# Two transformer layers on one core: polynomial and shifts moved from GpSimd to VectorE, shifts in pairs, single P buffers, a longer opening of layer 2

## The chip, the cores and the metric

The kernel runs on one core of a Trainium2 chip. The metric is the device time of one execution in microseconds, median of three runs. The core has five engines: TensorE (PE, matmuls; PEld its weight loads), VectorE (DVE), ScalarE (ACT), GpSimd (POOL) and SyncE (SP, which issues the DMAs).

## The reference

Two identical layers work on x of 2048 rows by 512, in bf16. Each is self-attention with 32 heads of 16 columns and then a feed-forward part of width 1792, both behind a layer norm without weights:

```
x = x + A(layernorm(x));  x = x + B(layernorm(x))        # twice
A(x): q, k, v = split(x @ wqkv);  softmax(q k^T / 4) v, heads joined, @ wo
B(x): gelu_tanh(x @ w1 + b1) @ w2 + b2
```

## The kernel before, in words

Keys and queries lie transposed, 128 columns (8 heads) to a block, and scores are computed transposed: 128 keys by 512 queries for one head. Such a **cell** fills one bank of PSUM (512 f32 a partition). There are 2 layers x 4 query chunks x 32 heads x 16 key tiles = 4096 cells. A **pass** is one query chunk, one block of columns and one of its two head halves, so four heads, and 64 cells where it takes all 16 key tiles; four matmuls of 32 rows each run side by side (`score`, L872). `qpad` (L860) masks the queries of a pass on GpSimd.

Most cells go to ScalarE: `exps` (L992) takes groups of three and two banks in turn and writes exp of them to a P buffer (L1004). Before, there are five P buffers of three cells, and a buffer is free when all its cells have been used. Some cells go to VectorE instead, only from four key tiles per layer (`KD`, L31): `dcell` (L962) turns a score into the bits of a bf16 number by one multiply-add to uint16 (L970). Three more copies of it, shifted by 32, 64 and 96 of these units, come from one shift of 512 elements (L973) and one of 1024 (L981 on VectorE, or for every third cell, if the planner sees GpSimd free, L978 there). The four are summed by four value matmuls with weighted copies of V (`VC`, made by `vcopies`, L845, on GpSimd), where a cell of ScalarE needs one. Before, five places (`DU`) hold the four forms of one cell each. `pvs` (L1020) runs the value matmuls of a pass into one bank, four heads side by side, and frees P buffers and places; `norm` (L603) transposes the sum, divides by its row of sums, and transposes back.

When a chunk's attention is done, `post` (L763) runs its output projection (`wo`, L637), a layer norm (`ln`, L473), seven pairs of hidden blocks (`hpair`, L692), the second product (`ytile`, L738) and, in layer 1, the next layer norm and the K, V, Q of layer 2 (`projections`, L575), all beside the attention of later chunks. A pair is 8 matmuls into two banks (L704), two evacuations (L717), then the tanh form of Gelu on 1024 elements: on GpSimd a square (L728), a scaling (L729) and a product (L731); tanh on ScalarE (L732); on VectorE +1 (L733) and the last product (L734). The last chunk of layer 2 uses ScalarE's own Gelu (L712). Pairs are released by the count of scored cells (`when`, L760: a share of `span`). Weights come in pieces of 256 KB through a ring of buffers `WR` (`wloads`, L664): two for the output projection, seven for the pairs, and six for K, V, Q of layer 2.

The order of passes (L802) is written out. Layer 2 opens with eight passes of its first chunk over 12 key tiles, whose sums wait in `PART`; then come the last four key tiles, which need K and V of the last 512 rows. So the last chunk's feed-forward part in layer 1 and its projections have to be done by then.

The order on each engine is fixed when the program is built: a planner (`_Sched`, L183) keeps a clock for each engine, and among steps that are ready takes the one with the lowest priority number. Each step has an estimated cost. Scores have 0, value matmuls 1, VectorE steps that read PSUM 0.4 at most, exponentials 6, cells of VectorE 9, feed-forward 10 to 15. On the chip each engine then works through its list in that order, and waits for semaphores where a step depends on another engine, or on its own engine's earlier step (TensorE's apart).

Of the kernel before, what the change touches and what calls it, by code (L numbers as in the profile page):

```python
# [5 lines left out]
ALU = mybir.AluOpType  # L6
# [28 lines left out]
PTLOW = 1  # L35
# [281 lines left out]
def bass_interleave_layers__mha_block__dense_activation_gelu__prompt_kernel(  # L317
# [15 lines left out]
    with ExitStack() as es:  # L333
# [17 lines left out]
        T["X2"] = sb([128, 2, 1024], F16, "x2")  # L351
        T["PT"] = sb([128, PT_RING, CELLS, 512], BF16, "pt")
        T["PART"] = [v[:, 0:8192].bitcast(F32).rearrange("p (g q) -> p g q", g=8) for v in vf[::-1]]
        T["DU"] = sb([128, DU, 4, 512], U16, "du")
# [52 lines left out]
DV = 0.62  # L407


class _Plan:  # L410
# [62 lines left out]
    def ln(self, c, dst, dkeys, prio):  # L473

        T = self.T
        tiles = range(4 * c, 4 * c + 4)
        sl = slice(4 * c, 4 * c + 4)
        for t in tiles:
            yield ("need", ("xready", t, self.phase[c]))
            yield _Op("dve", 0.6, lambda e, t=t: e.bn_stats(T["STATS"][:, t, :], T["X"][:, t, :]),  # L480
                      reads=["X.%d" % t], writes=["ST.%d" % t])
            yield _Op("dve", 0.1, lambda e, t=t: e.bn_aggr(T["MV"][:, t, :], T["STATS"][:, t, :]),
                      reads=["ST.%d" % t], writes=["MV.%d" % t])
# [12 lines left out]
    def ln_tile(self, c, t, dst, dkeys):  # L496
        T = self.T
        x = yield ("acq", "xln")
        yield _Op("dve", 0.22, lambda e: e.tensor_scalar(
# [103 lines left out]
    def norm(self, l, qc, g, b, part, final):  # L603
# [3 lines left out]
        key = "B.%d" % b  # L607
        if not final:
            yield _Op("dve", DV, lambda e: e.tensor_copy(T["PART"][l][:, g, :], pv), reads=[key],
                      writes=["PART.%d.%d" % (l, g)] + (["V0.%d" % k for k in range(self.NT)] + ["V01"] if l else []))  # L610
            yield ("rel", "pv", b)
            return
        xt = T["XT"]
        if part:
            yield _Op("dve", DV, lambda e: e.tensor_tensor(out=T["PART"][l][:, g, :], in0=T["PART"][l][:, g, :], in1=pv, op=ALU.add),
                      reads=[key, "PART.%d.%d" % (l, g)], writes=["PART.%d.%d" % (l, g)])
            yield ("rel", "pv", b)
            yield _Op("dve", 0.68, lambda e: e.transpose(xt[:, :], T["PART"][l][:, g, :]), reads=["PART.%d.%d" % (l, g)], writes=["XT"])
        else:
            yield _Op("dve", 0.70, lambda e: e.transpose(xt[:, :], pv), reads=[key], writes=["XT"])  # L620
            yield ("rel", "pv", b)
        x3 = xt[:, :].rearrange("p (k c) -> p k c", c=32)
        yield _Op("dve", 0.2, lambda e: e.reciprocal(T["RC"][:, :].rearrange("p (k o) -> p k o", o=1), x3[:, :, 16:17]),
# [5 lines left out]
        yield _Op("dve", 0.35, lambda e: e.tensor_tensor(  # L629
            out=o3, in0=x3[:, :, 0:16], in1=T["RC"][:, :, None].to_broadcast([128, 16, 16]), op=ALU.mult),  # L630
            reads=["XT", "RC"], writes=okey)
        if gt == 1:
            yield _Op("dve", 0.68, lambda e: e.transpose(T["OTN"][:, gb, :], T["OTT"][:, o, :]),
                      reads=["OTT.%d.0" % o, "OTT.%d.1" % o], writes=["OTN.%d" % gb])
            yield ("give", ("otn", l, qc, gb))
# [56 lines left out]
    def hpair(self, l, c, p):  # L692
# [40 lines left out]
        yield _Op("dve", 0.34, lambda e: e.tensor_scalar(x2, x2, 1.0, None, op0=ALU.add), reads=xk, writes=xk)  # L733
# [68 lines left out]
    def passes(self):  # L802


        NT = self.NT
        out = []
        for l in range(NL):
            cut = 4 if l == 0 else NT - 4
            out += [(l, 0, g, range(cut), False, False) for g in range(8)]
            out += [(l, 0, g, range(cut, NT), True, True) for g in range(8)]  # L810
            for qc in range(1, self.NQ):
                out += [(l, qc, g, range(NT), False, True) for g in range(8)]
        return out
# [9 lines left out]
    def setup_attention(self):  # L823
# [18 lines left out]
        self.ptleft = {}  # L842
        self.turn, self.lend = 0, 2
# [16 lines left out]
    def qpad(self):  # L860
        T = self.T
        for pi, (l, qc, g, kts, part, final) in enumerate(self.pas):
# [3 lines left out]
            yield _Op("pool", 0.9, lambda e, s=s, b=b, t=t, qc=qc: e.tensor_scalar(  # L866
# [42 lines left out]
    def scores(self):  # L909
        u = 0  # L910
        pools = self.s.pools
        while True:
# [12 lines left out]
            while len(work) < 4 and (pools["dbank"] or len(pools["misc"]) > KEEP) and pools["du"]:  # L925
                d = self.next_d(used)
                if d is None:
                    break
# [3 lines left out]
                extra.append((d, b, pools["du"].pop(0), home))  # L932
# [29 lines left out]
    def dcell(self, cell, b, du, home):  # L962


        T = self.T
        pi, kt, a = cell
        l, _, g = self.pas[pi][:3]
        D4 = T["DU"][:, du, :, :]
        key = ["DU.%d.%d" % (du, i) for i in range(4)]
        yield _Op("dve", 0.68, lambda e: e.tensor_scalar(D4[:, 0, :], self.bank(b), E_SCALE, E_BIAS, op0=ALU.mult, op1=ALU.add),  # L970
                  reads=["B.%d" % b], writes=key[:1])
        yield ("rel", "dbank", b)
        yield _Op("dve", 0.20, lambda e: e.tensor_scalar(D4[:, 1, :], D4[:, 0, :], SHIFT, None, op0=ALU.add),  # L973
                  reads=key[:1], writes=key[1:2])
        lo, hi = D4[:, 0:2, :].rearrange("p j q -> p (j q)"), D4[:, 2:4, :].rearrange("p j q -> p (j q)")
        self.turn = (self.turn + 1) % 3
        if self.turn == 0 and self.s.clock["pool"] < self.s.clock["dve"] + 0.1:
            yield _Op("pool", 1.36, lambda e: e.tensor_scalar(hi, lo, 1.0, 2.0 * SHIFT, op0=ALU.mult, op1=ALU.add),  # L978
                      reads=key[:2], writes=key[2:])
        else:  # L980
            yield _Op("dve", 0.34, lambda e: e.tensor_scalar(hi, lo, 2 * SHIFT, None, op0=ALU.add), reads=key[:2],  # L981
                      writes=key[2:])
        h = 8 * (g // 2) + 2 * a + (g % 2)
        j = KD[l].index(kt)
        for i in range(4):
            if i == 0:
                w, wk = T["V"][l][:, kt, h, 0:17], ["V%d.%d" % (l, kt), "V%d1" % l]
            else:
                w, wk = T["VC"][:, j, i - 1, 17 * h:17 * h + 17], ["VC.%d.%d" % (j, i - 1)]
            self.dq[(pi, a)].append((w, D4[:, i, :].bitcast(BF16), wk + key[i:i + 1], du if i == 3 else None, i == 3, kt))  # L990

    def exps(self):  # L992
        T = self.T
        u = 0
        while True:
            got = yield ("need", ("s", u))
            if got is None:
                break
            sl, cells = got
            r = yield ("acq", "pt")  # L1000
            n = len(cells)
            src = self.bank(SLOTS[sl][0], n)
            dst = T["PT"][:, r, 0:n, :].rearrange("p j q -> p (j q)")
            yield _Op("act", 0.065 + 0.4267 * n, lambda e, src=src, dst=dst: e.activation(  # L1004
                out=dst, in_=src, func=ACT.Exp, scale=0.25),
                reads=["B.%d" % b for b in SLOTS[sl][:n]], writes=["PT.%d" % r])
            self.ptleft[r] = n
            for j, (pi, kt, a) in enumerate(cells):
                l, _, g = self.pas[pi][:3]
                h = 8 * (g // 2) + 2 * a + (g % 2)  # L1010
                self.aq[(pi, a)].append((T["V"][l][:, kt, h, 0:17], T["PT"][:, r, j, :],
                                         ["V%d.%d" % (l, kt), "V%d1" % l, "PT.%d" % r], r, True, kt))
# [7 lines left out]
    def pvs(self):  # L1020
        T = self.T
        pools = self.s.pools
        for pi, (l, qc, g, kts, part, final) in enumerate(self.pas):
# [8 lines left out]
            def ready(cols=cols):  # L1032
# [4 lines left out]
                if not pools["pt"] and any(self.aq[k] for k in cols):  # L1037
# [3 lines left out]
            while any(self.pvleft[k] for k in cols):  # L1041
                yield ("cond", ready)
                fns, reads, rounds, back = [], [], 0, []
                while rounds < ROUNDS:
# [6 lines left out]
                    for k in wide:  # L1051
# [10 lines left out]
                        if buf is not None:  # L1062
                            back.append(("pt" if q is self.aq[k] else "du", buf))
                yield _Op("pe", ST + MM * (rounds - 1), fns, reads=reads, writes=["B.%d" % b])
                for pool, r in back:
                    if pool == "pt":
                        self.ptleft[r] -= 1
                        if self.ptleft[r]:
# [5 lines left out]
    def run(self):  # L1074
# [12 lines left out]
        s.pool("x2", range(2))  # L1087
# [44 lines left out]
```

## Time and profile before

| | |
|---|---|
| median of 3 runs | 1902.27 us (1902.13 to 1907.1) |
| profiled execution | 1901.61 us, of which 1899.6 us from first to last instruction (span) |
| busy: ScalarE, TensorE, VectorE, GpSimd | 1653.7, 1553.3, 1342.6, 540.3 us |
| mean granted TensorE clock | 0.889 of full |

A line of a group names the kernel's line, the engine, the operation, the tiles out<-in with their shapes and the count; then the busy time in us (overlaps counted once), the mean ns of one, and the idle time of the engine before them with what ended it. A row of the windows has the stretch, its length, the busy us of PE, PEld, DVE, ACT and POOL with their instructions in brackets, the granted clock, the DMA share and GB/s.

### The profile page before, as it was taken

The numbers are of one execution on the slowest core, as the hardware profiler recorded it, in microseconds if no ns is written. First come the engines' busy times: TensorE is split into PE (matmuls) and PEld (weight loads), VectorE is DVE, ScalarE is ACT, GpSimd is POOL, SyncE is SP. The second block draws the span as 40 slices with busy tenths as digits, with TensorE's granted clock in tenths as the row PEclk, the third lists the DMA queues.
The fourth block names the chain that finished last, engine by engine and source line by source line (L and its number), as shares of the span: only waits on it lengthen the run. The fifth ranks groups of instructions, "written<-read, shape, count | busy, mean of one in ns | idle before, by whom it ended". The sixth has DMA issues, their size and how long they took to land.

```text
span 1899.6 us, 28436 instructions
## 1 busy us (share of the span) xinstructions
PE 1553.3 (82%) x11548; PEld 372.8 (20%) x11548; DVE 1342.6 (71%) x2561; ACT 1653.7 (87%) x1458; POOL 540.3 (28%) x450
## 2 busy tenths in 40 slices
PE   7988887889869897787977968878887797877976
PEld 2211111122212121121211211212111121111212
DVE  6475678865897668867579544898668866788662
ACT  6999997899969998699987969979998799977992
POOL 3111125411262113522246101352214511254110
PEclk9997788899989999789988985989888798997998
DMA  5100000001100011000110010100001000010001
GB/s 144 34 1 1 1 23 28 12 1 45 29 28 7 17 30 35 28 1 12 45 28 23 1 43 3 29 28 12 7 12 34 17 10 4 18 29 17 12 1 44
DMA packets 85150, 42.45 MB, mean 22 GB/s; under 512 B 34589, under 2 KB 85022, under 8 KB 85022
## 3 DMA queue, kind: packets, MB, share of 16 engines
q1 hardware_dynamic: 85022, 40.65, 7.9%
q8 instruction: 92, 1.51, 0.3%
q14 instruction: 36, 0.29, 0.1%
HBM read 30.68 MB, written 2.10 MB: 17 GB/s over the span
## 4 chain that ended last, share of the span: by engine, by line
ACT 46%; PE 26%; DVE 24%; issue 2%; DMA 1%; POOL 0%; SPq 0%; POOLq 0%
ACT pt L1004 46%; PE ps L1058 10%; PE ps L880 8%; DVE du L970 5%; DVE du L973 5%; DVE du L981 4%; PE ps L704 3%; DVE g L717 3%; PE ps L745 3%; DVE x L733 2%; DVE g L734 2%; PE ps L549 1%; DMA xf<-xln 1%; DVE ott L629 1%; DVE xt L620 1%
## 5 line engine op out<-in xcount | busy, mean ns | idle before, releaser
L1004 ACT ACTIVATE pt<-ps 128x1536 bf16<-128x1536 f32 x1385 | 1595.8, 1293 | 186.7 <-PE ps L880 137.7
L880 PE MATMUL ps<-qp,kt 32*128 32x512 bf16 x4096 | 596.8, 420 | 220.6 <-ACT pt L1004 151.2
L970 DVE TENSOR_SCALAR du<-ps 128x512 uint16<-128x512 f32 x633 | 429.1, 684 | 280.1 <-PE ps L880 273.9
L1058 PE MATMUL ps<-pt,v 128*17 128x512 bf16 x3463 | 560.1, 421 | 7.3 <-ACT pt L1004 2.8
L978 POOL TENSOR_SCALAR du<-du 128x1024 uint16<-128x1024 uint16 x173 | 184.7, 1068 | 824.9 <-DVE du L973 813.0
L1058 PE MATMUL ps<-du,vc 128*17 128x512 bf16 x1899 | 389.5, 431 | 1.6 <-DVE du L973 1.3
L880 PEld LDWEIGHTS ps<-qp,kt 32*128 32x128 bf16 x4096 | 144.1, 92 | 860.2 <-ACT pt L1004 461.9
L981 DVE TENSOR_SCALAR du<-du 128x1024 uint16<-128x1024 uint16 x460 | 249.7, 546 | 8.3
L973 DVE TENSOR_SCALAR du<-du 128x512 uint16<-128x512 uint16 x633 | 246.0, 397 | 11.7
L704 PE MATMUL ps<-xf,wr 128*128 128x512 bf16 x448 | 146.8, 439 | 80.9 <-DVE g L717 59.8
L1058 PE MATMUL ps<-du,v 128*17 128x512 bf16 x633 | 198.2, 431 | 10.5 <-DVE xt L620 6.9
L866 POOL TENSOR_SCALAR qp<-q,mask 128x512 bf16<-128x512 bf16 x80 | 58.4, 731 | 297.6 <-PE ps L880 288.0
L1058 PEld LDWEIGHTS ps<-pt,v 128*17 128x17 bf16 x3463 | 104.5, 88 | 187.8 <-issue 156.1
L728 POOL TENSOR_TENSOR x<-g 128x1024 f16<-128x1024 bf16 x49 | 95.3, 1945 | 135.3 <-DVE g L717 127.5
L745 PE MATMUL ps<-w,g 128*128 128x512 bf16 x448 | 128.4, 390 | 3.0 <-DVE du L970 3.0
L731 POOL TENSOR_TENSOR x<-x,g 128x1024 f16<-128x1024 f16 x49 | 109.9, 2243 | 3.9
L717 DVE TENSOR_SCALAR g<-ps,hb1t 128x512 bf16<-128x512 f32 x98 | 72.7, 742 | 28.6 <-PE ps L704 28.1
L1058 PEld LDWEIGHTS ps<-du,vc 128*17 128x17 bf16 x1899 | 74.8, 91 | 88.2 <-issue 71.4
L704 PEld LDWEIGHTS ps<-xf,wr 128*128 128x128 bf16 x448 | 33.0, 103 | 163.9 <-issue 86.2
L729 POOL TENSOR_SCALAR x<-x 128x1024 f16<-128x1024 f16 x49 | 54.5, 1113 | 4.3
L733 DVE TENSOR_SCALAR x<-x 128x1024 f16<-128x1024 f16 x49 | 53.9, 1099 | 0.8 <-ACT x L732 0.8
L732 ACT ACTIVATE x<-x 128x1024 f16<-128x1024 f16 x49 | 51.8, 1057 | 1.6 <-POOL x L731 1.5
(57 smaller groups left out, 719.9 us busy)
## 6 DMA issues: line engine op xcount, KB each, us to landing
wr<-in_B_w_dram SPq DMA_DIRECT2D x56, 256.0 KB, 2.9
wr<-in_A_wqkv_dram SPq DMA_DIRECT2D x24, 256.0 KB, 2.7
wr<-in_A_wo_dram SPq DMA_DIRECT2D x16, 256.0 KB, 2.7
x<-in_A_x_dram SPq DMA_DIRECT2D x4, 512.0 KB, 8.5
out_dram<-x SPq DMA_DIRECT2D x16, 128.0 KB, 1.7
w<-in_B_w_dram SPq DMA_DIRECT2D x1, 1792.0 KB, 10.8
g<-in_A_wqkv_dram SPq DMA_DIRECT2D x3, 512.0 KB, 6.3
xf<-xln SPq DMA_TRANSPOSE x48, 2.4
```

The lines of the kernel that those rows point to most:

```text
L704: fns = [lambda e, dc=dc, j=j, pb=pb: e.matmul(pb, lhsT=T["WR"][:, w, 256 * dc + 128 * j:256 * dc + 128 * j + 128], rhs=T["XF"][:, dc, :], ...
L717: yield _Op("dve", DV, lambda e, fc=fc, pb=pb: e.tensor_scalar(T["G"][:, fc, :], pb, T["HB1T"][:, fc:fc + 1], 0.5, op0=ALU.add, op1=ALU.mult),
L728: yield _Op("pool", 2.2, lambda e: e.tensor_tensor(out=x2, in0=g2, in1=g2, op=ALU.mult), reads=gk, writes=xk)
L731: yield _Op("pool", 2.2, lambda e: e.tensor_tensor(out=x2, in0=x2, in1=g2, op=ALU.mult), reads=gk + xk, writes=xk)
L745: fns = [lambda e, fc=fc: e.matmul(pb, lhsT=T["G"][:, fc, q], rhs=T["W2"][:, fc, :], start=(fc == 0), stop=False) for fc in range(NFC)]
L880: return (lambda e: e.matmul(o, lhsT=lhsT, rhs=rhs, start=True, stop=True, tile_position=(32 * a, 0)), ["K%d.%d.%d" % (l, g // 2, kt // 4) ...
L970: yield _Op("dve", 0.68, lambda e: e.tensor_scalar(D4[:, 0, :], self.bank(b), E_SCALE, E_BIAS, op0=ALU.mult, op1=ALU.add), reads=["B.%d" % ...
L973: yield _Op("dve", 0.20, lambda e: e.tensor_scalar(D4[:, 1, :], D4[:, 0, :], SHIFT, None, op0=ALU.add), reads=key[:1], writes=key[1:2])
L978: yield _Op("pool", 1.36, lambda e: e.tensor_scalar(hi, lo, 1.0, 2.0 * SHIFT, op0=ALU.mult, op1=ALU.add), reads=key[:2], writes=key[2:])
L981: yield _Op("dve", 0.34, lambda e: e.tensor_scalar(hi, lo, 2 * SHIFT, None, op0=ALU.add), reads=key[:2], writes=key[2:])
L1004: yield _Op("act", 0.065 + 0.4267 * n, lambda e, src=src, dst=dst: e.activation(out=dst, in_=src, func=ACT.Exp, scale=0.25), reads=["B.%d" ...
L1058: fns.append(lambda e, o=o, lhsT=lhsT, rhs=rhs, a=a, st=not begun[a], sp=self.pvleft[k] == 0: e.matmul(o, lhsT=lhsT, rhs=rhs, start=st, st ...
```

## The change

The square, scaling and product of Gelu are issued on VectorE instead of GpSimd, and GpSimd makes no double shifts. VectorE's cells are gathered in pairs: `dfirst` does the multiply-add of each cell, and `dchain`, with priority 16, waits until two cells are there (or no second can come, or the exponentials lack P buffers), then does one shift for both and one double shift for both. There are three pair places. A place is free when both its cells have been used. P has 15 single buffers; `units` finds two or three free ones at equal steps, which one exponential writes, and each is freed by itself. `PTLOW` (free P buffers at which the value matmuls turn to ScalarE's cells first) counts singles now. Layer 2 opens with 12 passes over 12 key tiles (eight of chunk 0, four of chunk 1, whose sums lie in the first layer's K), then their last four tiles; its key tiles for VectorE are 0, 1, 2 and 12. The weight ring has three buffers. Some estimated costs of the planner are changed.

```diff
-CELLS = 3
-PT_RING = 5
+PT_RING = 15
-W_RING = 5
+W_RING = 3
-DU = 5
-KD = ((4, 5, 6, 7), (0, 1, 2, 3))
+X2_RING = 2
+DU = 3
+PAIR = 2
+LAST = 450
+EARLY = 4
+KD = ((4, 5, 6, 7), (0, 1, 2, 12))
-PTLOW = 1
+PTLOW = 3
...
+        T["PT"] = sb([128, PT_RING, 512], BF16, "pt")
+        T["PART1"] = T["K"][0][:, :, :].rearrange("p c s -> p (c s)").bitcast(F32).rearrange("p (g q) -> p g q", g=8)
+        T["DU"] = sb([128, DU, 4, PAIR, 512], U16, "du")
...
-        yield _Op("pool", 2.2, lambda e: e.tensor_tensor(out=x2, in0=g2, in1=g2, op=ALU.mult), reads=gk, writes=xk)
-        yield _Op("pool", 0.8, lambda e: e.tensor_scalar(x2, x2, 8.0 * C2, 2.0 * C1, op0=ALU.mult, op1=ALU.add),
+        yield _Op("dve", 0.62, lambda e: e.tensor_tensor(out=x2, in0=g2, in1=g2, op=ALU.mult), reads=gk, writes=xk)
+        yield _Op("dve", 0.36, lambda e: e.tensor_scalar(x2, x2, 8.0 * C2, 2.0 * C1, op0=ALU.mult, op1=ALU.add),
                   reads=xk, writes=xk)
-        yield _Op("pool", 2.2, lambda e: e.tensor_tensor(out=x2, in0=x2, in1=g2, op=ALU.mult), reads=gk + xk, writes=xk)
+        yield _Op("dve", 0.62, lambda e: e.tensor_tensor(out=x2, in0=x2, in1=g2, op=ALU.mult), reads=gk + xk, writes=xk)
...
+        out = run(0, 0, range(8), range(4), False, False) + run(0, 0, range(8), range(4, NT), True, True)
+        for qc in range(1, self.NQ):
+            out += run(0, qc, range(8), every, False, True)
+        out += run(1, 0, range(8), most, False, False) + run(1, 1, range(EARLY), most, False, False)
+        out += run(1, 0, range(8), rest, True, True) + run(1, 1, range(EARLY), rest, True, True)
+        out += run(1, 1, range(EARLY, 8), every, False, True)
...
-                self.span[(l, c)] = 384 if (l, c) == (0, self.NQ - 1) else 512
+                self.span[(l, c)] = LAST if (l, c) == (0, self.NQ - 1) else 260 if (l, c) == (1, 0) else 512
...
+                if self.open is None:
+                    self.open = {"du": pools["du"].pop(0), "cells": [], "full": False}
+                    yield ("spawn", self.dchain(self.open), 16)
+                pair = self.open
+                pair["cells"].append(d)
...
+    def dfirst(self, pair, j, b):
+        u = self.T["DU"][:, pair["du"], 0, j, :]
+        yield _Op("dve", 0.68, lambda e: e.tensor_scalar(u, self.bank(b), E_SCALE, E_BIAS, op0=ALU.mult, op1=ALU.add),
+                  reads=["B.%d" % b], writes=["DU.%d.0.%d" % (pair["du"], j)])
+        pair["done"] = pair.get("done", 0) + 1
+        yield ("rel", "dbank", b)
...
+    def dchain(self, pair):
+        T = self.T
+        cells, du = pair["cells"], pair["du"]
+        yield ("cond", lambda: len(cells) == PAIR or pair["full"] or self.starved)
+        if self.open is pair:
+            self.open = None
+        yield ("cond", lambda: pair.get("done", 0) == len(cells))
+        n = len(cells)
+        U = T["DU"][:, du, :, :, :]
...
+        yield _Op("dve", 0.08 + 0.14 * n, lambda e: e.tensor_scalar(U[:, 1, 0:n, :], U[:, 0, 0:n, :], SHIFT, None, op0=ALU.add),
+                  reads=key[0], writes=key[1])
+        yield _Op("dve", 0.08 + 0.28 * n, lambda e: e.tensor_scalar(U[:, 2:4, 0:n, :], U[:, 0:2, 0:n, :], 2 * SHIFT, None, op0=ALU.add),
+                  reads=key[0] + key[1], writes=key[2] + key[3])
+        self.duleft[du] = n
...
-            r = yield ("acq", "pt")
             n = len(cells)
+            if self.units(n) is None:
+                self.starved = n
+                yield ("cond", lambda n=n: self.units(n) is not None)
+                self.starved = 0
+            run = self.units(n)
+            for r in run:
+                yield ("take", ("pt", r))
+            step = run[1] - run[0] if n > 1 else 1
+            src = self.bank(SLOTS[sl][0], n).rearrange("p (j q) -> p j q", j=n)
+            dst = T["PT"][:, run[0]:run[-1] + 1:step, :]
...
-                if not pools["pt"] and any(self.aq[k] for k in cols):
+                if self.starved and any(self.aq[k] for k in cols):
                     return True
```

## Rows read from the trace of the kernel before

**Rows 1.** The page: span, busy shares, chain, one group.

```profile
span 1899.6 us, 28436 instructions
PE 1553.3 (82%) x11548; PEld 372.8 (20%) x11548; DVE 1342.6 (71%) x2561; ACT 1653.7 (87%) x1458; POOL 540.3 (28%) x450
ACT 46%; PE 26%; DVE 24%; issue 2%; DMA 1%; POOL 0%; SPq 0%; POOLq 0%
L1004 ACT ACTIVATE pt<-ps 128x1536 bf16<-128x1536 f32 x1385 | 1595.8, 1293 | 186.7 <-PE ps L880 137.7
```

**Rows 2.** Windows, attention alone and layer 2's opening: busy us (instructions), clock, DMA.

```profile
590.00:745.00 155.00, 135.27 (x1093) 33.56 (x1091) 105.07 (x231) 153.22 (x136) 29.85 (x30) 0.98 0.09 23
1100.00:1232.00 132.00, 104.66 (x702) 23.72 (x699) 74.82 (x152) 113.03 (x100) 23.35 (x24) 0.78 0.10 27
```

**Rows 3.** The same view of seven feed-forward stretches: first, last, sum.

```profile
283.00:355.00 72.00, 52.90 (x369) 12.03 (x367) 62.43 (x93) 53.29 (x48) 35.88 (x23) 0.88 0.10 28
1670.00:1745.00 75.00, 54.11 (x375) 12.24 (x371) 66.55 (x95) 55.16 (x49) 40.39 (x25) 0.84 0.09 26
sum 530.00, PE 398.35 PEld 88.97 DVE 469.83 ACT 396.38 POOL 280.03; mean PE 56.91 PEld 12.71 DVE 67.12 ACT 56.63 POOL 40.00
```

**Rows 4.** Single lines over the run: shortest, median, longest in ns.

```profile
L973 DVE TENSOR_SCALAR du<-du x633: 221/293/2206, 102.1 to 1841.3; 128x512 uint16<-128x512 uint16 x159
L981 DVE TENSOR_SCALAR du<-du x460: 366/427/2339, 102.4 to 1841.5; 128x1024 uint16<-128x1024 uint16 x154
L733 DVE TENSOR_SCALAR x<-x x49: 409/460/2334, 306.3 to 1746.6; 128x1024 f16<-128x1024 f16 x49
L734 DVE TENSOR_TENSOR g<-x,g x49: 671/683/2264, 307.3 to 1747.1; 128x1024 bf16<-128x1024 f16 x49
```

**Rows 5.** Groups of VectorE in 283 to 355 us: busy us, mean ns, idle before.

```profile
L973 DVE TENSOR_SCALAR du<-du 128x512 uint16<-128x512 uint16 x20 | 13.1, 654 | 0.4
L981 DVE TENSOR_SCALAR du<-du 128x1024 uint16<-128x1024 uint16 x20 | 17.0, 850 | 0.4
L733 DVE TENSOR_SCALAR x<-x 128x1024 f16<-128x1024 f16 x6 | 3.8, 637 | 0.2 <-ACT x L732 0.2
```

**Rows 6.** Groups of VectorE over the run, the same columns.

```profile
L973 DVE TENSOR_SCALAR du<-du 128x512 uint16<-128x512 uint16 x633 | 246.0, 397 | 11.7
L981 DVE TENSOR_SCALAR du<-du 128x1024 uint16<-128x1024 uint16 x460 | 249.7, 546 | 8.3
L733 DVE TENSOR_SCALAR x<-x 128x1024 f16<-128x1024 f16 x49 | 53.9, 1099 | 0.8 <-ACT x L732 0.8
```

**Rows 7.** Groups of VectorE in 1050 to 1100 us.

```profile
L970 DVE TENSOR_SCALAR du<-ps 128x512 uint16<-128x512 f32 x20 | 13.8, 689 | 15.3 <-PE ps L880 15.2
L973 DVE TENSOR_SCALAR du<-du 128x512 uint16<-128x512 uint16 x20 | 5.8, 292 | 0.6
L981 DVE TENSOR_SCALAR du<-du 128x1024 uint16<-128x1024 uint16 x13 | 5.5, 424 | 0.3
```

**Rows 8.** Timeline in the fifth stretch: start us, duration us.

```profile
1267.72 2.17 POOL L731 TENSOR_TENSOR x<-x,g 128x1024 f16<-128x1024 f16 x1
1267.84 2.33 DVE L733 TENSOR_SCALAR x<-x 128x1024 f16<-128x1024 f16 x1
```

**Rows 9.** Timeline at the transition: ScalarE's first exponentials after its two waits.

```profile
1112.18 2.37 ACT L1004 ACTIVATE pt<-ps 128x1024 bf16<-128x1024 f32 x2 [9.86 <-PE ps L880]
1124.98 5.97 ACT L1004 ACTIVATE pt<-ps 128x1536 bf16<-128x1536 f32 x5 [6.16 <-PE ps L1058]
```

**Rows 10.** Waits of ScalarE over the run: us, times, longest.

```profile
ACT pt L1004 <- PE ps L1058: 44.2, 36, 6.2
```

**Rows 11.** Timeline of the closing feed-forward part: its first matmuls.

```profile
1868.24 14.78 PE L704 MATMUL ps<-xf,wr 128*128 128x512 bf16 x56 [13.27 <-DMA xf<-xln]
```

**Rows 12.** DMA issues: KB each, us to landing.

```profile
wr<-in_B_w_dram SPq DMA_DIRECT2D x56, 256.0 KB, 2.9
```

More of the change, by code (lines that the diff above doesn't have):

```diff
@@ L607, in norm @@
         key = "B.%d" % b
+        if qc == 0:
+            pt, pk = T["PART"][l][:, g, :], "PART.%d.%d" % (l, g)
+            over = ["V0.%d" % k for k in range(self.NT)] + ["V01"] if l else []
+        else:
+            pt, pk = T["PART1"][:, g, :], "PART1.%d" % g
+            over = ["K0.%d.%d" % (g // 2, c) for c in range(self.NQ)]
         if not final:
-            yield _Op("dve", DV, lambda e: e.tensor_copy(T["PART"][l][:, g, :], pv), reads=[key],
-                      writes=["PART.%d.%d" % (l, g)] + (["V0.%d" % k for k in range(self.NT)] + ["V01"] if l else []))
+            yield _Op("dve", DV, lambda e: e.tensor_copy(pt, pv), reads=[key], writes=[pk] + over)
             yield ("rel", "pv", b)
@@ L805, in passes, with run @@
         NT = self.NT
[L806 to L812, printed above, removed]
+        def run(l, qc, gs, kts, part, final):
+            return [(l, qc, g, kts, part, final) for g in gs]
+        every, most, rest = range(NT), range(NT - 4), range(NT - 4, NT)
+        out = run(0, 0, range(8), range(4), False, False) + run(0, 0, range(8), range(4, NT), True, True)
[4 more added lines that the diff above has]
+        out += run(1, 1, range(EARLY, 8), every, False, True)
+        for qc in range(2, self.NQ):
+            out += run(1, qc, range(8), every, False, True)
         return out
@@ L924, in scores @@
             extra = []
-            while len(work) < 4 and (pools["dbank"] or len(pools["misc"]) > KEEP) and pools["du"]:
+            while len(work) < 4 and (pools["dbank"] or len(pools["misc"]) > KEEP) and (self.open or pools["du"]):
                 d = self.next_d(used)
                 if d is None:
+                    if self.open:
+                        self.open["full"] = True
+                        self.open = None
                     break
@@ L931, in scores @@
                 b = pools[home].pop(0)
-                extra.append((d, b, pools["du"].pop(0), home))
+                if self.open is None:
[3 more added lines that the diff above has]
+                pair["cells"].append(d)
+                extra.append((d, b, pair, len(pair["cells"]) - 1))
+                if len(pair["cells"]) == PAIR:
+                    self.open = None
                 work.append((d, b))
@@ L947, in scores @@
             self.scored += len(work)
-            for d, b, du, home in extra:
+            for d, b, pair, j in extra:
                 self.nd += 1
-                yield ("spawn", self.dcell(d, b, du, home), DPRIO)
+                yield ("spawn", self.dfirst(pair, j, b), DPRIO)
             for qs in free:
@@ L960, in scores @@
             yield ("rel", "misc", b)
-    def dcell(self, cell, b, du, home):
-        T = self.T
[L966 to L990, printed above, removed]
@@ L992, in exps, with units @@
+    def units(self, n):
+        free = sorted(self.s.pools["pt"])
+        for i in range(len(free) - n + 1):
+            if n == 1:
+                return free[:1]
+            for j in range(i + 1, len(free)):
+                run = [free[i] + (free[j] - free[i]) * k for k in range(n)]
+                if all(r in free for r in run):
+                    return run
+        return None
     def exps(self):
@@ L1062, in pvs @@
                         if buf is not None:
-                            back.append(("pt" if q is self.aq[k] else "du", buf))
+                            back.append(buf)
                 yield _Op("pe", ST + MM * (rounds - 1), fns, reads=reads, writes=["B.%d" % b])
                 for pool, r in back:
-                    if pool == "pt":
-                        self.ptleft[r] -= 1
-                        if self.ptleft[r]:
+                    if pool == "du":
+                        self.duleft[r] -= 1
+                        if self.duleft[r]:
                             continue
@@ L1086, in run @@
         s.pool("w", range(W_RING))
-        s.pool("x2", range(2))
+        s.pool("x2", range(X2_RING))
         self.setup_attention()
```

56 lines of the change are left out of this document (31 added, 25 removed).

## The prediction

> **What bounds the kernel now.** I read the busy shares first. ScalarE is busy 1653.7 of 1899.6 us and does the exponentials of 4096 score cells less those that VectorE takes: 3463 cells in 1595.8 us, 0.461 us a cell [rows 1]. The chain of waits gives ScalarE 46%, TensorE 26%, VectorE 24%, so no engine bounds all of the run [rows 1]. The windows say where each does. In a stretch with attention alone (590 to 745 us) ScalarE is busy 153.22 of 155 us: it is the bound, with VectorE at 68% [rows 2]. In the seven stretches where a feed-forward part runs beside attention (530 us together) ScalarE is busy only 396.38 us, so 133.6 us are lost; VectorE is busy 469.83 us, 89%, TensorE 398.35, and GpSimd 280.03 [rows 3]. The rest of ScalarE's idle time is the start, the transition between the layers, the closing feed-forward part, and small gaps.
>
> Then I asked what VectorE's time is made of. The medians of the shift, double shift and +1 lines are 0.293, 0.427 and 0.460 us, their longest 2.2 to 2.3 us [rows 4]. In the first stretch the means of the three are 0.654, 0.850 and 0.637 us [rows 5], over the run 0.397, 0.546 and 1.099 us [rows 6]; in 1050 to 1100, without a polynomial, 0.292 and 0.424 us [rows 7]. The same instruction on the same shape is slower beside the polynomial. The timeline shows one: GpSimd's product of 2.17 us starts at 1267.72, VectorE's +1 of 0.46 us starts 0.12 us behind it and takes 2.33 us, to 1270.17, just behind GpSimd's end at 1269.89 [rows 8]. So VectorE's 89% holds much waiting on GpSimd. Call it the toll: 20 x 0.423 + 20 x 0.361 + 6 x 0.177 = 16.8 us in the first stretch [rows 4, 5]; the same for the seven gives 16.8, 17.4, 19.7, 21.2, 17.3, 18.3, 18.7, together 129 us, of 152 us in the run (633 x 0.104 + 460 x 0.119 + 49 x 0.639) [rows 4, 6].
>
> **The change part by part.** *Polynomial to VectorE.* Each of 49 pairs gets a square and a product like the last product, 0.683 us, and a two-operation scaling that no row shows on this engine and size: 0.460 us as the +1, at most 0.683 us as a two-tensor form [rows 4]. I take 0.460, the nearest in kind: 1.82 us (bound 2.05), seven to a stretch, 12.7 us added (14.4).
>
> *Shifts to VectorE, in pairs.* 173 double shifts come over; the seven stretches hold 160 shifts and 142 double shifts on VectorE, so 18 of them, 2.6 x 0.427 = 1.1 us in each. A pair needs one shift of 1024 elements, 0.427 us, and one of 2048, which no row shows: doubling 512 to 1024 adds 0.134 us, so 0.427 + 2 x 0.134 = 0.695 us, at most 2 x 0.427 = 0.854 [rows 4]. For one cell that is 0.56 us (bound 0.64) where it was 0.72: with 23 cells in a stretch, 3.6 us less (bound 1.8).
>
> *The toll.* GpSimd keeps the Q padding, value copies and powers. Outside the stretches it did these and its share of the shifts, and the means were at the medians [rows 7], so I take the 18.5 us a stretch as gone; a rest of 1 to 2 us stands against what two smaller lines give back that I left out.
>
> VectorE in a stretch is then 67.1 - 18.5 + 12.7 + 1.1 - 3.6 = 58.8 us. ScalarE keeps its 56.6 and TensorE its 56.9 [rows 3]: three engines nearly tie. If the fullest one is as busy as VectorE is now, 89%, the stretch is 66 us; at ScalarE's 99% of rows 2 it is 59.5 us. I take 65, near the first, since three orders fixed by hand now meet: 10.7 us less than 75.7, seven times: 75 us. Bounds: 59.5 gives 113 us; 73.5 (80% busy, three ties that disturb each other) gives 15 us.
>
> *Twelve opening passes.* ScalarE waits 9.86 us and 6.16 us at the transition, until K and V of the last 512 rows are there [rows 9]. Four more passes of 48 cells put 192 cells, at 1899.6/4096 = 0.46 us some 89 us, ahead of that need; the wait lasts until 1125, some 25 us. I take 15 of 16 us back (bounds 0 and 16). Their price, four more PSUM copies and four adds of about 0.69 us as another PSUM read [rows 7], 5.5 us of VectorE, is hidden: it was busy 74.82 of 132 us there [rows 2]. If that cover went, they would cost 5.5 us. What is late next is the first chunk's feed-forward part of layer 2, spread over 260 cells instead of 512; its VectorE work is the same, and I cost it at nothing (bound: 10 us, a stretch's saving lost).
>
> *P buffers freed singly.* ScalarE waits 44.2 us for value matmuls to free a buffer [rows 10]; 6.2 us of it are the transition's, and most of the rest lies in the stretches and is counted there. I take 6 us beside those (bounds 0 and 38). The exponential has the same size; its output only steps between units.
>
> *Three weight buffers instead of five.* A load lands 2.9 us after issue; the closing 56 matmuls take 14.78 us, 2.1 us for a pair [rows 11, 12]. With three buffers pair n+3 is loaded when pair n is done, two pairs or 4.2 us ahead, so it just fits: +1 us (bounds 0 and 5). SP's queue has the transposes and stores behind a load that waits for its buffer; in the stretches seven pairs share 75.7 us, 11 us each, which hides it.
>
> *How many cells VectorE takes.* The planner decides; each is worth 0.461 us of ScalarE. Six places in three pairs for five single ones, but both places of a pair come free together and the first cell waits for the second; cells come every 2.5 us (20 in 50 us) [rows 7], so a hold of up to 5 x 2.5 = 12.5 us grows by some 2.5 to 3 us, and 6/15.3 is 2% under 5/12.5. Against that, key tile 12 gives the last-tile passes of layer 2, which had none, some VectorE cells. I keep 633, with 100 either way as bounds.
>
> Sum: 75 + 15 + 6 - 1 = 95 us off the span, 1804.6 us; 2.0 us lie around the span (1901.61), and the median is 0.7 us above that execution: 1807 us.
>
> **A rule that speaks against it.** The Trainium skill, Perfetto Trace Analysis, Optimizing Scalar/DVE Operations, says that with VectorE saturated it may pay to give work to ScalarE or even GpSimd, and adds that between GpSimd and VectorE it might not help, as they share a port. By its first half, moving work onto an engine at 89% loses (the slower rival below); by its second the toll goes and my sum stands. Rows 8 lean to the second half.
>
> **The rivals.** *VectorE saturates (slower).* Place: the seven stretches. If the slow shifts were due to something that stays, such as the instructions' own order, no toll comes back: 67.1 + 12.7 + 1.1 - 3.6 = 77.3 us, at 89% 86.9 us, 11.2 us longer, seven times 78; less 20 for the other parts: 1902 + 58 = 1960 us. It decides where less than about 10 us of the 18.5 come back. For it: shifts stand last in priority, behind the polynomials, and value matmuls wait for them in TensorE's fixed order. Against: rows 7 and 8.
>
> *Pairs hold their places too long.* 100 cells fewer on VectorE put 46 us on ScalarE: 1853 us; 200 fewer would eat the gain. For it: a cell's place now waits for a partner and for both cells' matmuls. Against: VectorE's room between the stretches, 32% [rows 2].
>
> *VectorE takes more.* Without the toll 100 more cells cost 100 x (0.689 + 0.56) = 125 us of VectorE, which the attention stretches have, and take 46 us off: 1761 us. For it: the same 32%. Against: in 1050 to 1100 VectorE waits 15 us for scores to come, so banks, places and order limit it, not its time [rows 7].
>
> *TensorE binds the stretch.* It is busy 56.9 us of 75.7 at a granted clock of 0.88 in the first stretch and 0.84 in the last [rows 3]; if its order keeps the stretch at 75.7 us, 20 us remain: 1882 us. Against: it works 87% of the time in 590 to 745 [rows 2].
>
> **How the numbers follow.** Forecast 0.55, with 1770 to 1840 as its own range; fewer cells 0.16, more cells 0.13, TensorE 0.08, saturation 0.08. The range 1750 to 1875 holds the forecast, most of both cell cases, and leaves out TensorE's case and saturation. A measurement here tells 0.3% (5.7 us) from no change. Faster 0.88: the forecast, more cells, TensorE's case, and most of fewer cells; same 0.04: its far end; slower 0.08: saturation.
>
> **What would show it.** In the profile after: GpSimd busy below 110 us; means of the shift and +1 lines at their medians inside the stretches; ScalarE at 85 to 90% there instead of 75%, and each stretch about 65 us long; no wait above 3 us at the transition; 530 to 730 cells on VectorE. The prediction is wrong if the shift lines stay stretched with GpSimd idle, if VectorE is above 97% busy in the stretches while ScalarE stays near 75%, or if the cell count leaves those bounds.

## The result, and the profile after

The median fell from 1902.2 to 1739.89 us (1737.37 to 1743.08), a ratio of 0.9146, 95% interval 0.9119 to 0.9173: 162 us, where 95 were forecast, and 10 us below the low end of the range. The profiled execution took 1738.12 us.

The page of after, with the lines that answer [rows 1] and the count of cells on VectorE (L987 is the multiply-add, L1051 the exponential):

```profile
span 1736.3 us, 27780 instructions
PE 1482.5 (85%) x11465; PEld 373.0 (21%) x11605; DVE 1251.7 (72%) x2308; ACT 1631.3 (94%) x1451; POOL 109.1 (6%) x134
...
ACT 72%; PE 18%; issue 5%; DVE 3%; DMA 1%; POOL 0%; POOLq 0%; SPq 0%
...
L1051 ACT ACTIVATE pt<-ps 128x1536 bf16<-128x1536 f32 x1378 | 1581.3, 1339 | 48.6 <-PE ps L893 29.7
L987 DVE TENSOR_SCALAR du<-ps 128x512 uint16<-128x512 f32 x652 | 441.3, 686 | 285.0 <-PE ps L893 279.4
```

ScalarE is busy 1631.3 us, 22.4 less, and idle 105.0 of 1736.3 us where it was idle 245.9. It heads 72% of the chain of waits instead of 46%. GpSimd fell from 540.3 to 109.1 us. The seven feed-forward stretches, found again by their 14 evacuations each, in the view of [rows 3], the first and the sum:

```profile
283.00:341.00 58.00, 50.28 (x384) 12.99 (x383) 52.38 (x97) 57.44 (x53) 1.75 (x2) 0.97 0.11 33
...
sum 382.00, PE 322.52 PEld 84.60 DVE 356.09 ACT 373.29 POOL 10.82; mean PE 46.08 PEld 12.09 DVE 50.87 ACT 53.33 POOL 1.55
```

They take 382 us and hold 870 scored cells (score matmuls in the same windows); before, they took 530 us and held 922. At the pace of the stretches themselves the 52 cells more would take 23 us, so 530 us became about 405. The windows of before hold 91 of the 98 evacuations, those of after all of them, so the fall is a little larger still. ScalarE is busy 98% (it was 75%), VectorE 93%, TensorE 84%. Attention alone is as it was in [rows 2], with VectorE at 67%:

```profile
590.00:690.00 100.00, 88.47 (x672) 21.00 (x681) 67.11 (x130) 98.29 (x87) 6.68 (x6) 0.91 0.11 27
```

VectorE's groups in the first stretch, answering [rows 5], with the new square (L736) and scaling (L737):

```profile
L1006 DVE TENSOR_SCALAR du<-du 128x2048 uint16<-128x2048 uint16 x9 | 6.1, 681 | 0.0
L736 DVE TENSOR_TENSOR x<-g 128x1024 f16<-128x1024 bf16 x7 | 4.7, 676 | 0.0
L1004 DVE TENSOR_SCALAR du<-du 128x1024 uint16<-128x1024 uint16 x9 | 4.1, 464 | 0.0
L741 DVE TENSOR_SCALAR x<-x 128x1024 f16<-128x1024 f16 x7 | 2.9, 420 | 0.6 <-ACT x L740 0.6
L737 DVE TENSOR_SCALAR x<-x 128x1024 f16<-128x1024 f16 x7 | 2.9, 419 | 0.0
```

The +1 line is at 0.420 us where its mean was 0.637, the shift of 1024 at 0.464, the pair's double shift of 2048 elements at 0.681. The two-operation scaling costs 0.419, as much as the +1, and the square 0.676. Waits of ScalarE over the run, answering [rows 10]; the longest wait for a score is 1.6 us and for a value matmul 2.0 us, so the transition's two waits of [rows 9] are gone:

```profile
ACT pt L1051 <- PE ps L893: 29.7, 45, 1.6
ACT g L720 <- PE ps L712: 23.3, 14, 19.5
ACT pt L1051 <- PE ps L1104: 16.1, 20, 2.0
```

In the closing feed-forward part, answering [rows 11], a run of matmuls waited 0.35 us for weights:

```profile
1712.67 3.68 PE L712 MATMUL ps<-xf,wr 128*128 128x512 bf16 x15 [0.35 <-DMA wr<-in_B_w_dram]
```

### The profile page after: what moved, and what is told of

It reads as the page before. It is cut to its first block, busy times and chain, and to the rows that moved or that the text cites. A ratio compares the mean times of both kernels' runs of the same rounds, so it can differ in the third digit from the quotient of the medians.

```text
span 1736.3 us, 27780 instructions
## 1 busy us (share of the span) xinstructions
PE 1482.5 (85%) x11465; PEld 373.0 (21%) x11605; DVE 1251.7 (72%) x2308; ACT 1631.3 (94%) x1451; POOL 109.1 (6%) x134
## 4 chain that ended last, share of the span: by engine, by line
ACT 72%; PE 18%; issue 5%; DVE 3%; DMA 1%; POOL 0%; POOLq 0%; SPq 0%
ACT pt L1051 70%; PE ps L1104 8%; PE ps L893 6%; ACT x L740 2%; PE ps L753 1%; PE ps L712 1%; PE ps L553 1%; DVE du L987 1%; DVE du L1006 0%; DVE du L1004 0%; DVE g L725 0%; DMA xf<-xln 0%; PE ps L550 0%; DMA x<-in_A_x_dram 0%; DVE stats L484 0%
## 5 line engine op out<-in xcount | busy, mean ns | idle before, releaser
L1051 ACT ACTIVATE pt<-ps 128x1536 bf16<-128x1536 f32 x1378 | 1581.3, 1339 | 48.6 <-PE ps L893 29.7
L987 DVE TENSOR_SCALAR du<-ps 128x512 uint16<-128x512 f32 x652 | 441.3, 686 | 285.0 <-PE ps L893 279.4
L1104 PE MATMUL ps<-du,vc 128*17 128x512 bf16 x1956 | 370.2, 421 | 0.6 <-ACT pt L1051 0.5
L1006 DVE TENSOR_SCALAR du<-du 128x2048 uint16<-128x2048 uint16 x333 | 227.1, 684 | 5.7
L1104 PE MATMUL ps<-du,v 128*17 128x512 bf16 x652 | 153.1, 422 | 1.4 <-DVE xt L628 0.8
L1004 DVE TENSOR_SCALAR du<-du 128x1024 uint16<-128x1024 uint16 x333 | 139.7, 424 | 6.0
L712 PE MATMUL ps<-xf,wr 128*128 128x512 bf16 x405 | 117.0, 389 | 23.4 <-DMA xf<-xln 13.1
L760 DVE TENSOR_TENSOR x<-x,ps 128x512 bf16<-128x512 bf16 x32 | 21.9, 684 | 37.8 <-PE ps L755 37.7
L573 DVE CAST v<-ps 128x512 bf16<-128x512 f32 x32 | 22.2, 693 | 34.8 <-PE ps L550 30.2
L484 DVE BATCH_NORM_STATS2 stats<-x 128x6 f32<-128x512 bf16 x64 | 42.7, 669 | 3.4 <-DMA x<-in_A_x_dram 3.4
L753 PEld LDWEIGHTS ps<-w,g 128*128 128x128 bf16 x448 | 30.2, 98 | 67.3 <-issue 47.8
L1104 PEld LDWEIGHTS ps<-du,v 128*17 128x17 bf16 x652 | 33.0, 89 | 50.5 <-issue 29.4
```

The source lines that it names most:

```text
L484: yield _Op("dve", 0.66, lambda e, t=t: e.bn_stats(T["STATS"][:, t, :], T["X"][:, t, :]), reads=["X.%d" % t], writes=["ST.%d" % t])
L712: fns = [lambda e, dc=dc, j=j, pb=pb: e.matmul(pb, lhsT=T["WR"][:, w, 256 * dc + 128 * j:256 * dc + 128 * j + 128], rhs=T["XF"][:, dc, :], ...
L753: fns = [lambda e, fc=fc: e.matmul(pb, lhsT=T["G"][:, fc, q], rhs=T["W2"][:, fc, :], start=(fc == 0), stop=False) for fc in range(NFC)]
L987: yield _Op("dve", 0.68, lambda e: e.tensor_scalar(u, self.bank(b), E_SCALE, E_BIAS, op0=ALU.mult, op1=ALU.add), reads=["B.%d" % b], write ...
L1004: yield _Op("dve", 0.08 + 0.14 * n, lambda e: e.tensor_scalar(U[:, 1, 0:n, :], U[:, 0, 0:n, :], SHIFT, None, op0=ALU.add), reads=key[0], w ...
L1006: yield _Op("dve", 0.08 + 0.28 * n, lambda e: e.tensor_scalar(U[:, 2:4, 0:n, :], U[:, 0:2, 0:n, :], 2 * SHIFT, None, op0=ALU.add), reads=k ...
```

## The experiments

Theory T: GpSimd's long instructions held VectorE's, VectorE's lost time was the stretches' lost time, and with it gone the fixed order holds. Rival B: the single P buffers, the pairs and the opening gave most of it. Rival L: the polynomial cost time by its own length on GpSimd, in the chain to tanh.

**The polynomial alone, in the kernel before (b_poly).**

```diff
-        yield _Op("pool", 2.2, ... in0=g2, in1=g2 ...   # and the scaling and the product, likewise
+        yield _Op("dve", 0.62, ... in0=g2, in1=g2 ...
```

> Before with the three polynomial instructions on VectorE and nothing else changed (double shifts of every third cell stay on GpSimd, five triple P buffers, old opening). Theory T (GpSimd's long instructions hold VectorE's, and with that gone the fixed order holds on the chip): ScalarE's idle time in the seven feed-forward stretches falls from 133 us to below 50, time 1780 to 1820 us. Rival B (single P buffers, pairs and the opening give most of the gain, the toll is a side effect): 1850 us or more, ScalarE below 85% busy in the stretches.

Measured: 1777.05 us, ratio 0.9344 (0.9313 to 0.9376): 126 of the 162 us from three instructions alone, and 3 us below the low end of T's range. Its busy line; a window from a stretch, one from the transition, and the sum of all seven stretches (each from just before the first evacuation to the last product); VectorE's groups over the run:

```profile
span 1770.7 us, 28238 instructions
PE 1483.0 (84%) x11396; PEld 370.8 (21%) x11530; DVE 1237.0 (70%) x2657; ACT 1647.8 (93%) x1461; POOL 331.3 (19%) x336
```

```profile
725.00:750.00 25.00, 22.77 (x176) 6.10 (x176) 25.00 (x56) 25.00 (x24) 4.01 (x3) 1.00 0.15 43
1025.00:1050.00 25.00, 15.88 (x70) 3.63 (x68) 6.00 (x11) 7.38 (x7) 1.38 (x2) 0.68 0.17 43
...
sum 427.00, PE 362.43 PEld 93.51 DVE 403.31 ACT 418.18 POOL 88.02; mean PE 51.78 PEld 13.36 DVE 57.62 ACT 59.74 POOL 12.57
```

```profile
L981 DVE TENSOR_SCALAR du<-du 128x1024 uint16<-128x1024 uint16 x421 | 188.3, 451 | 5.9
L973 DVE TENSOR_SCALAR du<-du 128x512 uint16<-128x512 uint16 x627 | 181.1, 297 | 9.1
...
L733 DVE TENSOR_SCALAR x<-x 128x1024 f16<-128x1024 f16 x49 | 24.6, 505 | 0.0
```

VectorE has 49 x 3 instructions more and is still 105.6 us less busy than before. The two shift lines fell from 0.397 and 0.546 to 0.297 and 0.451 us [rows 6], the +1 from 1.099 to 0.505. In the stretches ScalarE is busy 418.18 of 427 us, 98%, with the old buffers, single cells and a third of the double shifts still on GpSimd: 9 us idle, where T asked for less than 50. VectorE is at 94% beside it. Only the transition (1025 to 1050) is open as before. B falls for the stretches.

How VectorE's slow lines reached ScalarE is in TensorE's waits, before and then in b_poly: in before it waits for VectorE to read two PSUM tiles, the evacuations of the pairs (L717) and the multiply-adds of the cells (L970).

```profile
PE ps L704 <- DVE g L717: 59.8, 38, 4.8
PE ps L880 <- DVE du L970: 41.2, 38, 4.9
```

```profile
PE ps L704 <- DVE g L717: 7.3, 16, 1.0
PE ps L880 <- DVE du L970: 3.1, 6, 1.0
```

With these, ScalarE's waits for scores fell from 137.7 us [rows 1] to 41.2 in b_poly. Rival L finds next to nothing in before: ScalarE waited 1.5 us in all for the polynomial's product.

```profile
ACT x L732 <- POOL x L731: 1.5, 1, 1.5
```

**The polynomial back on GpSimd, in the kernel after (a_polypool).**

```diff
-        yield _Op("dve", 0.62, ... in0=g2, in1=g2 ...   # likewise the other two
+        yield _Op("pool", 2.2, ... in0=g2, in1=g2 ...
```

> After with the three polynomial instructions back on GpSimd, all else as after. T: shift and +1 lines are stretched to 0.6 us and more again beside the polynomial, 1830 to 1890 us. B: the single buffers and the new opening stand, no more than 1790 us.

Measured: 1852.91 us, ratio 0.9734 (0.9702 to 0.9767), 113 us above after. All the other parts of the change then give 49 us of 162. The run counts for its time alone: its values are not the reference's, for a reason that is left open, though it does the same work, with 147 instructions moved and 16 cells more on VectorE. In its first stretch the +1 takes 1.329 us on average and the shift 0.864, as T said, and over the run ScalarE waits 113.7 us for scores and 3.3 us for the polynomial.

**GpSimd busy beside the polynomial, with nothing waiting for it (a_pt14 and a_toll).** The scratch tile needs room, so both have 14 P buffers.

```diff
-PT_RING = 15
+PT_RING = 14
# a_toll only, spawned where a pair's square is issued:
+        y, z = T["Y"][:, :], T["W2"][:, 0:2, :].rearrange("p a q -> p (a q)")[:, 0:704]
+        for c in (1.4,) * 4:
+            yield _Op("pool", c, lambda e: e.tensor_tensor(out=y, in0=z, in1=z, op=ALU.mult), reads=["W2"], writes=["Y"])
```

> After with 14 P buffers instead of 15; the control for the next kernel. Both theories: 1745 to 1770 us, a little above after.

> As the kernel with 14 P buffers, in the same order on TensorE, ScalarE, VectorE and SyncE, but GpSimd gets four two-tensor multiplies of 704 elements beside each of the 49 polynomials; they read the second weight, write a scratch tile, and nothing waits for them. T: VectorE's shift, scaling and product lines get longer beside them, and the time rises by 60 to 140 us over the control. Rival L (the polynomial on GpSimd cost time by its own length in the chain from product to tanh, not by holding VectorE): within 10 us of the control.

Measured: 1755.65 us for the control and 1884.88 with the idle multiplies: 129 us, as much as the whole gain of the polynomial's move, from instructions on which nothing depends. Pages of the control and of a_toll:

```profile
span 1764.9 us, 27769 instructions
PE 1501.5 (85%) x11457; PEld 375.6 (21%) x11593; DVE 1252.3 (71%) x2312; ACT 1637.0 (93%) x1452; POOL 107.9 (6%) x134
```

```profile
span 1879.9 us, 27965 instructions
PE 1536.3 (82%) x11457; PEld 376.5 (20%) x11593; DVE 1387.7 (74%) x2312; ACT 1645.4 (88%) x1452; POOL 411.0 (22%) x330
```

Between these two executions, whose spans lie 115 us apart, VectorE's busy time grew by 135.4 us with the same 2312 instructions in the same order. One window and the sum of the seven stretches, control and then a_toll:

```profile
300.00:325.00 25.00, 20.67 (x159) 5.39 (x160) 24.48 (x45) 25.00 (x24) 0.69 (x1) 1.00 0.13 38
...
sum 399.00, PE 335.86 PEld 86.52 DVE 361.85 ACT 385.44 POOL 13.19; mean PE 47.98 PEld 12.36 DVE 51.69 ACT 55.06 POOL 1.88
```

```profile
300.00:325.00 25.00, 16.13 (x102) 3.07 (x100) 23.95 (x29) 15.19 (x14) 11.74 (x8) 0.73 0.08 22
...
sum 529.00, PE 389.18 PEld 88.68 DVE 494.85 ACT 397.78 POOL 310.89; mean PE 55.60 PEld 12.67 DVE 70.69 ACT 56.83 POOL 44.41
```

The stretches grow from 399 to 529 us and ScalarE's share falls from 97% to 75%, that of [rows 3], with VectorE at 94%: GpSimd alone makes the loss again. Square, product and multiply-add, control and then a_toll (the added lines shift the numbers by two and more):

```profile
L736 DVE TENSOR_TENSOR x<-g 128x1024 f16<-128x1024 bf16 x49 | 34.1, 696 | 0.0
L739 DVE TENSOR_TENSOR x<-x,g 128x1024 f16<-128x1024 f16 x49 | 33.6, 686 | 0.4
L987 DVE TENSOR_SCALAR du<-ps 128x512 uint16<-128x512 f32 x648 | 439.6, 687 | 303.7 <-PE ps L893 296.8 <-PE ps L755 4.2
```

```profile
L738 DVE TENSOR_TENSOR x<-g 128x1024 f16<-128x1024 bf16 x49 | 56.6, 1155 | 0.0
L741 DVE TENSOR_TENSOR x<-x,g 128x1024 f16<-128x1024 f16 x49 | 53.8, 1098 | 0.4
L995 DVE TENSOR_SCALAR du<-ps 128x512 uint16<-128x512 f32 x648 | 438.9, 686 | 286.7 <-PE ps L901 280.6 <-PE ps L763 4.2
```

The multiply-adds, which read PSUM, keep their 0.687 us, and so do the evacuations (0.746 and 0.740). All the lines that grow read and write SBUF alone, above all the shifts, the lines of the polynomial and the product in `norm`.

And the timeline of one case in a_toll: three multiplies run in a row from 325.93; the scaling (0.420 us alone) takes 1.47 us, the product (0.686) 1.73.

```profile
325.93 5.05 POOL L752 TENSOR_TENSOR y<-w 128x704 f16<-128x704 bf16 x3
326.54 1.47 DVE L739 TENSOR_SCALAR x<-x 128x1024 f16<-128x1024 f16 x1
328.04 1.73 DVE L741 TENSOR_TENSOR x<-x,g 128x1024 f16<-128x1024 f16 x1
```

L, as it was put, falls: no result of GpSimd is late here, and the Q padding behind the multiplies on GpSimd costs TensorE no more than in the control (waits of 1.2 and 1.0 us). What is shown is that running instructions on GpSimd is enough. But the time is not lost at the same place as in before. Here VectorE's own product comes late, and ScalarE waits for it in front of tanh, 3.7 us in the control and 72.6 in a_toll:

```profile
ACT x L742 <- DVE x L741: 72.6, 35, 6.3
```

In before it waited 1.5 us there, and most for scores. So the toll is the same, but that 129 us come so near to 126 is in part chance.

**The same elements in quarter-length instructions (a_toll_short).**

```diff
-        for c in (1.4,) * 4:       # 704 elements each
+        for c in (0.35,) * 16:     # 176 elements each
```

> As the kernel with the four GpSimd multiplies of 704 elements beside each polynomial, but sixteen of 176 elements: the same elements in quarter-length instructions, order of the other engines unchanged. If an instruction of VectorE waits for the end of the one GpSimd instruction that runs (T): waits shrink to about a quarter each, and the time lies 20 to 60 us above the control with 14 P buffers, 1755.65 us. If it is GpSimd's busy time that counts, or each one holds VectorE again (rival): 90 us or more above it.

Measured: 1813.84 us (1806.89 to 1820.98), 58 above the control, at the upper end of T's range and under half of 129. The busy line, the square, and GpSimd's multiplies here and in a_toll:

```profile
PE 1519.3 (84%) x11593; PEld 374.0 (21%) x11593; DVE 1336.8 (74%) x2312; ACT 1642.1 (91%) x1452; POOL 569.6 (32%) x918
...
L738 DVE TENSOR_TENSOR x<-g 128x1024 f16<-128x1024 bf16 x49 | 43.7, 892 | 0.0
```

```profile
L752 POOL TENSOR_TENSOR y<-w 128x176 f16<-128x176 bf16 x784 | 464.2, 592 | 59.9
```

```profile
L752 POOL TENSOR_TENSOR y<-w 128x704 f16<-128x704 bf16 x196 | 301.9, 1540 | 14.2
```

GpSimd is busy longer (464.2 against 301.9 us) and yet costs less. An instruction is 0.592 us long against 1.540, a share of 0.38, and the square's excess over the control is 0.196 us against 0.459, a share of 0.43. The other lines fall less: VectorE's busy time is 84.5 us above the control's, against 135.4, a share of 0.62. An estimate from these rows, waits as long as the one instruction in the way and as frequent as GpSimd is busy, gives 0.38 x 464.2/301.9 = 0.59. So a short instruction holds VectorE for less, but the more of them there are, the more often.

**The opening (a_open8).**

```diff
-EARLY = 4
+EARLY = 0
-KD = ((4, 5, 6, 7), (0, 1, 2, 12))
+KD = ((4, 5, 6, 7), (0, 1, 2, 3))
# and the old shares: 384 for LAST, 512 for the first chunk of layer 2
```

> After with the opening of layer 2 as before: eight passes, key tiles 0 to 3, the old shares of scored cells (384 and 512). Theory T: the wait at the transition is back, about 16 us of ScalarE, and some ten cells go back to ScalarE: 1755 to 1765 us. Rival B (the opening is a large part of the gain): 1775 us or more.

Measured: 1749.7 us, ratio 0.9194 (0.9169 to 0.9219): 10 us above after (8 above its second measurement, 1742.07 us, below), less than T said. VectorE takes 641 cells, 11 fewer, as T said. The wait at the transition comes back shorter, 4.7 us at the longest:

```profile
ACT pt L1051 <- PE ps L1104: 30.4, 27, 4.7
```

**P in blocks of three (a_triples).**

```diff
-        s.pool("pt", range(PT_RING))
+        s.pool("pt", range(PT_RING // 3))    # a block is freed when its last cell is used; PTLOW = 1
```

> After with the same 15 P places handed out and freed in five blocks of three, and the planner's threshold at one block. T: a small part, 1745 to 1760 us (fewer cells on VectorE and a few waits for P). Rival B (single buffers absorb the jitter that kept ScalarE at 75% in the stretches): 1780 us or more, ScalarE's share in the stretches below 90%.

Measured: 1748.56 us, 9 above after (6 above its second measurement), as T said. VectorE takes 631 cells instead of 652 (the count of matmuls on the unweighted V), and 21 x 0.459 = 9.6 us of exponentials go back to ScalarE, while its waits for scores and value matmuls, 42.9 us, are no longer than the 45.8 of after: single buffers pay by letting VectorE take more cells, not by filling the stretches. One buffer fewer costs as much or more: 16 us in the control with 14 above.

```profile
L1105 PE MATMUL ps<-du,v 128*17 128x512 bf16 x631 | 165.2, 417 | 0.6 <-ACT pt L1052 0.4
```

**Single cells instead of pairs (a_pair1).**

```diff
-DU = 3
-PAIR = 2
+DU = 6
+PAIR = 1
```

> After with six places of one cell instead of three of two (same memory), so each cell has its own two shifts. VectorE then spends 0.72 us instead of 0.56 on a cell's shifts but a place is free sooner. T: 1735 to 1755 us, VectorE takes 20 to 30 cells more. Rival P (pairing is what lets VectorE keep up in the stretches): 1770 us or more with VectorE at its limit there.

Measured: 1757.35 us, 17 above after (15 above its second measurement): just over T's range and clear of P's. VectorE takes 677 cells, as T said, yet ScalarE waits longer, 69.7 us against 45.8 for scores and value matmuls:

```profile
ACT pt L1051 <- PE ps L893: 36.7, 51, 1.6
ACT pt L1051 <- PE ps L1104: 33.0, 65, 2.0
```

So pairing is worth more than its share of cells, but why these waits grow is not settled: more work on VectorE (1337.0 us busy against 1251.7) and another order came together.

**The shifts alone on top of the polynomial (b_poly_shift).**

```diff
-        if self.turn == 0 and self.s.clock["pool"] < self.s.clock["dve"] + 0.1:
+        if False:
```

> Before with the polynomial and every double shift on VectorE, cells still single, old buffers and opening. T: a double shift of 1.05 us on GpSimd holds VectorE little, since it follows on VectorE's own work; 173 x 0.427 = 74 us of VectorE work come over, where it has room: 1765 to 1795 us, about the same as with the polynomial alone. If the shifts on GpSimd cost much by the port: 1750 us or less.

Measured: 1780.73 us, ratio 0.9358 (0.9329 to 0.9386), the same as with the polynomial alone. Moving the double shifts gives nothing by itself. T's reason was wrong, though: 206 double shifts came over, 88 us of work at 0.425 us, and VectorE's busy time grew by only 25.4 us, with 9 cells fewer. On GpSimd they had held VectorE too (the +1 fell from 0.505 to 0.418 us), but no time hung on it.

**A faster version (x_q5), beside the changed kernel on the same chip (after_again).**

```diff
-QUEUE = 4
+QUEUE = 5
-DWIDE = 2
+DWIDE = 1
```

> The changed kernel once more, on the same chip as the next ones: 1735 to 1745 us.

> After with two thresholds of the planner changed: the second spare bank is left to VectorE's cells until more than five steps wait for one (four in after), and value matmuls start with one head at hand where pair places are short (two in after). ScalarE is 97 to 99% busy from start to end now, so only fewer cells on it help. 669 cells on VectorE instead of 652, each worth 0.459 us: 8 us, so 1728 to 1736 us. If VectorE's 97% in the stretches is a bound of its own: no change.

Measured: 1742.07 us for the changed kernel, ratio 0.9153 (0.913 to 0.9177), and 1730.57 us for this one, ratio 0.9091 (0.9067 to 0.9116). It beats both; 8 us were expected, 11.5 measured.

```profile
PE 1506.4 (87%) x11656; PEld 373.5 (22%) x11656; DVE 1272.4 (74%) x2347; ACT 1623.0 (94%) x1444; POOL 106.4 (6%) x134
...
L987 DVE TENSOR_SCALAR du<-ps 128x512 uint16<-128x512 f32 x669 | 453.2, 686 | 293.3 <-PE ps L893 289.3
```

VectorE takes 669 cells, and ScalarE is 8.3 us less busy than in after.

## Why the prediction was wrong, point by point

*The reading was right.* VectorE's stretched lines were the toll, GpSimd was the cause, and the stretches were where it counted; b_poly shows it with three instructions moved, a_toll with the order of the other engines unchanged.

*The step that failed* is the size of the main term: "If the fullest one is as busy as VectorE is now, 89%, the stretch is 66 us; at ScalarE's 99% of rows 2 it is 59.5 us. I take 65, near the first, since three orders fixed by hand now meet." The stretches came out at 405 us for the same cells, 57.9 us each instead of 65, and gave 125 us, not 75: past even the other bound of that passage, 59.5 us and 113 us. The 89% was VectorE's share while the toll held it. Without the toll the fullest engine is ScalarE, whose 56.6 us by the prediction's own sum take 57.8 us at the measured 98%. The loss that I took for one that would stay came from the toll too: VectorE read PSUM late, TensorE waited 101 us for it in before and 10.4 in b_poly, and ScalarE waited for scores; a_toll makes a loss of the same size in an order that fills ScalarE without it. That "three orders fixed by hand now meet" cost next to nothing here: over the stretches of b_poly ScalarE is at 98% with VectorE at 94%, and from 725 to 750 us both are busy 25.00 of 25 us.

*Prices.* Polynomial: 0.676 + 0.419 + 0.68 us, close to the 1.82 taken. The pair's double shift 0.68 to 0.695 us, as worked out. VectorE's load, 58.8 us a stretch by the sum, came to 50.9, or at most 53.9 for the cells of before (50.9 x 922/870, as if all of it went by cells): 8% under or more. Some 2.5 us of that are two lines which the toll stretched as well and which the sum left out, the last product (5.86 to 4.53 us a stretch) and the product in `norm`, L629 before (1.93 to 0.71); the rest is open.

*Transition:* the waits of 16 us went, as forecast; but taking the opening out of after costs only 10 us, with a longest wait of 4.7 us, so in the changed kernel the opening alone is not worth the 15. *P buffers:* 6 forecast, 6 to 9 measured, by another way (cells). *Weights:* waits of 0.35 us and, on weight loads, 0.84 us in the closing part, for +1. *Cells:* 652 against the 633 kept, 19 x 0.459 = 9 us, inside its bounds. *Terms together:* 125 for the stretches, 16 for the transition and 9 for the cells make 150 of the span's 163.3 us; I have no term for the other 13; a part may be the evacuations that the windows of before leave out, the rest is open.

*The rivals.* "VectorE takes more" came in part, with 19 cells instead of 100. "VectorE saturates" did not come: VectorE is at 93% in the stretches, and ScalarE is full. TensorE did not bind them either (84% busy), and pairs did not cost cells against before (652 for 633). By the Trainium skill's advice in Perfetto Trace Analysis, Optimizing Scalar/DVE Operations, the clause that counted is the second, that giving GpSimd work from VectorE might not help as they share a port. The Trainium skill, SBUF — State Buffer, Who interferes with whom, says that of VectorE in a two-port mode and GpSimd, whichever issues first gets the shared pair for its whole instruction, and the other is blocked. The timeline of a_toll agrees for the scaling: three multiplies of 5.05 us together started at 325.93, the first ends, as an estimate, a third of that later, near 327.61, and the scaling ends at 328.01, its own 0.420 us behind.

## What to carry to other kernels

Compare an instruction's mean with its median, stretch by stretch, before deciding what an engine's busy share means: VectorE lines at twice their median beside running GpSimd instructions were waiting here, and work given to GpSimd to unload VectorE may cost it more than it saves (here 88 us of polynomial on VectorE bought 126 us). Lines that read PSUM did not stretch, and so can serve as the control. When a disturbance is removed, size the gain by the fullest engine at the share that undisturbed stretches reach, not by the share that the disturbed ones had. Work that has to stay on GpSimd did less harm in short instructions here (58 us instead of 129).

## What the runs showed that I had not expected

Multiplies on GpSimd that nobody waits for cost 129 us, more than all the other parts of the change give together (49 us). The mean granted clock of TensorE rose from 0.889 to 0.929 with the time saved, though its work hardly changed; in a_toll it is 0.896. No run separates what the faster TensorE itself gave. It does not set the time alone: in the profiled execution of a_toll_short the clock, 0.928, is above the control's 0.923, and the span is 40 us longer. Two operations with constants on 1024 f16 elements take VectorE 0.419 us, as long as one (0.420).
